# The last 64 rows of the first MLP matrix: one transfer of 128 partitions, or one of 96 and four of 8

## The chip, the cores and the metric

The kernel runs on one core of one Trainium2 chip. The metric is the device time of one execution in microseconds (us), the median of several runs. The profile is one further execution, recorded by the hardware profiler.

## What is computed

The reference mixes two blocks for a batch of 8 tokens with 576 features, all in bf16. A is attention for one decode step: 32 query heads on 16 key and value heads of 128, over the last 2048 of 8192 cached positions. B is an MLP with a hidden width of 4608. A gate per token weighs the two.

```
q = (x @ wq)                            # wq 576 x 4096
p = softmax(q . k / sqrt(128))          # k: last 2048 positions of the cache
a = (p . v) @ wo                        # wo 4096 x 576
h = gelu(layernorm(x) @ w1 + b1)        # w1 576 x 4608
b = h @ w2 + b2                         # w2 4608 x 576
g = sigmoid((x * gate_w).sum(-1))
out = g * a + (1 - g) * b
```

The two caches' windows are 134 MB of the 154 MB that the kernel reads; the weights are the rest.

## The kernel before

**Loads.** Every load is issued by SP (SyncE), on one DMA queue, in an order written out in the code by `after=` links. First come the last 64 rows of wq, its first 512 rows, x, gate_w, b1 and b2 (lines 407 to 413). Then comes w1: the 512 first rows as `d_w1m` (line 416; 128 partitions of 36,864 bytes), and the 64 last rows as `d_w1r` (line 417). For the latter each row is cut into two halves, which makes 128 pieces of 2304 elements, 4608 bytes, one per partition of the tile `w1_r`. Behind these stand the loads of the attention: 16 units, each with a K load and a V load of 4 MB (line 618), into four buffer slots used in turn. Slots 1 and 2 are free from the start, so K0 and K1 are issued right behind w1; V0 goes to slot 0, which holds wq until `q_pe` has read it, and K2 to slot 3, which holds w1 until `h_pe` has read it. At the end come w2 in four pieces (line 865) and wo in two (line 836).

**Semaphores.** A load adds 16 to its semaphore when it has landed in full. Both w1 loads use the semaphore "w1"; `h_pe`, the matmuls of the hidden layer (line 551, with its own lines 543 and 501), waits for both.

**Compute.** `q_pe` multiplies x by wq, and VectorE and ScalarE turn q into a block form. `mask0` (line 687, emitted at lines 685 and 175) writes the first unit's mask to PSUM, and `h_pe` makes the hidden layer. For each unit, VectorE transposes K (line 718), TensorE makes scores (lines 732 and 175), VectorE takes the maximum (line 645), ScalarE the exponential (line 649), and TensorE multiplies by V (lines 755 and 188). After all units the group of matmuls at line 579 adds the products with w2 and wo into one bank; line 900 copies it out and line 903 stores it.

**The order on each engine** is set by a planner (`schedule`, line 62). It holds a cost for each operation and a model of the loads, and always takes the operation that could start first. In the model, loads of at least 65,536 bytes follow each other at 428e3 bytes per us and land 1.8 us after their last byte. A smaller one on SP lands 1.8 us after what was booked so far, and books nothing itself:

```
                if op.nbytes < 65536:
                    op.t1 = (max(est + 0.4, dma_free) if op.eng == "sp" else est + 0.4) + self.DMA_LAT
                else:
                    start = max(est + 0.4, dma_free)
                    dma_free = start + op.nbytes / self.DMA_BW
                    op.t1 = dma_free + self.DMA_LAT
```

In that model h_pe can start at 25.71, and mask0, which needs the last of the q copies (line 537), at 25.44. These are the planner's own figures, which order the instructions and measure nothing.

Of the kernel before, what the change touches and what calls it, by code (L numbers as in the profile page):

```python
# [38 lines left out]
class _Plan:  # L39
# [16 lines left out]
    def dma(self, eng, fn, semkey, nbytes, deps=(), name=None, after=(), prio=0):  # L56
        op = _Op(eng, fn, deps, name, self.DMA_ISSUE, after=after, is_dma=True, dma_sem=semkey, nbytes=nbytes, prio=prio)
        op.idx = len(self.all)
        self.all.append(op)
        return op  # L60
# [134 lines left out]
def build_kernel(nc, A_x, A_k_cache, A_v_cache, A_wq, A_wo, B_x, B_w1, B_b1, B_w2, B_b2, gate_w, out):  # L195
# [3 lines left out]
    F = B_w1.shape[1]  # L199
# [25 lines left out]
    with ExitStack() as es:  # L225
# [134 lines left out]
        w1_r = RAW[:, W1O + 4 * F:W1O + 4 * F + F // 2]  # L360
# [19 lines left out]
        add, dma = P.add, P.dma  # L380
# [33 lines left out]
        dx = [d_x]  # L414
        db = [d_b1]
        d_w1m = dma("sp", lambda e: e.dma_start(w1_m.rearrange("p t c -> p (t c)"), B_w1[0:512, :].rearrange("(p t) c -> p (t c)", t=4)), "w1", 512 * F * 2, name="d_w1m", after=[d_b2])
        d_w1r = dma("sp", lambda e: e.dma_start(w1_r, B_w1[512:576, :].rearrange("k (s c) -> (k s) c", s=2)), "w1", 64 * F * 2, name="d_w1r", after=[d_w1m])  # L417
        dw1 = [d_w1m, d_w1r]


        def spread(name, src):
# [171 lines left out]
        M_CUTS = [[24], [8, 3, 1]]  # L593
        stream += [("M", 0), ("W", 0), ("W", 1), ("M", 1)]

        last_dma = [d_w1r]
        slot_free = [[o_qp], [], [], [o_hp], [o_qp, o_hp]]
        n_slot = [0]
        qk_hist, pe_hist, dve_ops = [], [], {}
# [313 lines left out]
def bass_gated_mix__sliding_block_cached__mixer_channel_mlp__decode_kernel(  # L913
    nc: bass.Bass,
    A_x: bass.AP,
    A_k_cache: bass.AP,
    A_v_cache: bass.AP,
    A_wq: bass.AP,
    A_wo: bass.AP,
    B_x: bass.AP,  # L920
    B_w1: bass.AP,
    B_b1: bass.AP,
    B_w2: bass.AP,
    B_b2: bass.AP,
    gate_w: bass.AP,
    out: bass.AP,
):
    build_kernel(nc, A_x, A_k_cache, A_v_cache, A_wq, A_wo, B_x, B_w1, B_b1, B_w2, B_b2, gate_w, out)
# [28 lines left out]
```

## Time and profile before

| what | before |
|---|---|
| median of three runs | 364.71 us (364.57 to 365.15) |
| the profiled execution, its time and its span | 364.42 us, 363.0 us |
| TensorE, VectorE, ScalarE, GpSimd busy | 81%, 64%, 46%, 6% of the span |
| bytes moved, mean rate | 154.45 MB, 425 GB/s |
| K loads: count, KB each, median from issue to landing | 16, 4096 KB, 28.7 us |
| V loads: the same | 16, 4096 KB, 25.5 us |
| d_w1m: issue, KB | 3.00 us, 4608 KB |
| d_w1r: issue, KB, issue to landing | 3.40 us, 576 KB, 23.0 us |

The page of the profile gives times in us from the start of the span. Its second part cuts the span into 40 slices and gives for each the busy tenths of an engine; the DMA line is the mean of the core's sixteen DMA engines. Its third part lists the DMA queues. The other views used below are the chain of work that ended last, in order of time; the instructions in order of time (start, duration, engine, line, operation, and in brackets how long the engine stood idle before it and what released it); and the view of one line of the code. The trace also holds two lists below these views: each DMA packet with its start, duration and size, and each step that a DMA made on a semaphore.

### The profile page before, as it was taken

Reading aid. Unit: us, or ns where it says so; the run is one execution under the profiler, and the core shown is the slowest. Engines: PE = TensorE matmul, PEld = TensorE weight load, DVE = VectorE, ACT = ScalarE, POOL = GpSimd, SP = SyncE. Lnnn points to the kernel's source line nnn. Section 1 sums busy time; section 2 is a strip of 40 time slices with the busy share of each in tenths; the row PEclk is TensorE's granted clock in tenths of the full one; section 3 lists DMA queues with packets and bytes.
Section 4 is the critical chain, followed back from the end, with each engine's and each line's share of the span. In section 5 each row is a group of like instructions: output and inputs, shape, how many; then the busy total and the mean of one; then the engine's idle time right before and its main releaser. Section 6 shows DMA issues by size and latency. Waiting matters only on the chain.

```text
span 363.0 us, 4802 instructions
## 1 busy us (share of the span) xinstructions
PE 295.1 (81%) x1935; PEld 125.4 (35%) x1423; DVE 231.6 (64%) x166; ACT 168.6 (46%) x130; POOL 22.9 (6%) x52
## 2 busy tenths in 40 slices
PE   0455357999999969898897979897979699999875
PEld 0121000435252615242433416150615143436742
DVE  0453989576666694929385768566675949295720
ACT  1022106655647464564637373838374636655000
POOL 9032030000010000000100000000000000003000
PEclk9999596999999999999999999999999989999999
DMA  8999999999999999999999999999999999999996
GB/s 347 436 437 406 459 408 459 408 459 408 454 412 455 412 455 410 452 415 451 415 451 415 446 419 448 419 448 417 448 419 448 419 446 419 448 419 444 409 434 249
DMA packets 6118, 154.45 MB, mean 425 GB/s; under 512 B 702, under 2 KB 856, under 8 KB 1244
## 3 DMA queue, kind: packets, MB, share of 16 engines
q1 hardware_dynamic: 6092, 154.30, 98.8%
q8 instruction: 8, 0.13, 0.1%
q14 instruction: 2, 0.02, 0.0%
q10 hardware_dynamic: 16, 0.00, 0.0%
HBM read 154.29 MB, written 0.01 MB: 425 GB/s over the span
## 4 chain that ended last, share of the span: by engine, by line
DMA 54%; PE 21%; DVE 21%; issue 2%; SPq 1%; ACT 0%
DMA arena<-in_A_k_cache_dram 48%; DVE arena L718 17%; PE ps L175 9%; PE ps L188 6%; DMA arena<-in_B_w_dram 6%; PE ps L732 3%; PE ps L755 2%; DVE arena L668 2%; DVE arena L645 1%; DVE arena L794 1%; PE ps L579 0%; PE ps L685 0%; DVE arena L561 0%; DVE arena L900 0%; SPq L417 0%
## 5 line engine op out<-in xcount | busy, mean ns | idle before, releaser
L718 DVE STREAM_TRANSPOSE arena<-arena 128x4096 f32<-128x4096 f32 (+1 forms) x34 | 141.7, 4175 | 24.3 <-DMA arena<-in_A_k_cache_dram 24.3
L674 ACT ACTIVATE arena<-arena 32x2048 bf16<-32x2048 bf16 x60 | 114.5, 1908 | 72.8 <-DVE arena L668 44.7
L175 PE MATMUL ps<-arena 128*128 128x512 bf16 (+3 forms) x524 | 134.7, 397 | 12.6 <-DVE arena L718 9.6
L188 PE MATMUL ps<-arena 128*128 x840 | 109.8, 277 | 6.9 <-issue 0.7
L188 PEld LDWEIGHTS ps<-arena 128*128 x840 | 81.3, 97 | 34.4 <-issue 19.1
L645 DVE TENSOR_REDUCE arena<-ps 128x1 f32<-128x2048 f32 x16 | 36.7, 2292 | 53.3 <-PE ps L175 53.3
L732 PE MATMUL ps<-arena 128*128 128x512 bf16 x122 | 48.2, 395 | 20.0 <-DVE arena L718 18.3
L732 PEld LDWEIGHTS ps<-arena 128*128 128x128 bf16 x128 | 12.5, 98 | 133.0 <-issue 75.2
L649 ACT ACTIVATE arena<-ps,arena 128x2048 bf16<-128x2048 f32 x16 | 40.6, 2538 | 0.5
L646 ACT ACTIVATE arena<-arena 128x1 f32<-128x1 f32 x16 | 3.2, 203 | 62.8 <-DVE arena L645 62.8
L755 PE MATMUL ps<-arena 128*128 128x256 bf16 x184 | 25.3, 273 | 1.2 <-DVE arena L663 1.1
L755 PEld LDWEIGHTS ps<-arena 128*128 128x128 bf16 x184 | 16.8, 98 | 19.1 <-issue 14.7
L668 DVE STREAM_TRANSPOSE arena<-arena 128x1024 f32<-128x1024 f32 x15 | 18.1, 1205 | 2.9 <-ACT arena L649 2.9
L579 PE MATMUL ps<-arena 128*8 128x288 bf16 (+1 forms) x140 | 9.6, 286 | 4.0 <-DMA arena<-in_A_wo_dram 3.3
L739 POOL MEMSET arena<- 128x4096 f32 x1 | 3.5, 3512 | 148.2 <-PE ps L175 148.2
L629 POOL COPY arena<-arena 32x64 bf16<-32x64 bf16 x16 | 3.7, 230 | 123.6 <-PE ps L175 122.7
L901 ACT ACTIVATE arena<-ps 8x288 bf16<-8x288 f32 x1 | 0.4, 401 | 19.5 <-PE ps L579 19.5
L422 DVE COPY arena<-arena 8x128 bf16<-8x128 bf16 x2 | 0.5, 229 | 13.9 <-DMA arena<-in_A_x_dram 13.9
L579 PEld LDWEIGHTS ps<-arena 128*8 128x8 bf16 (+1 forms) x140 | 5.8, 86 | 9.5 <-DMA arena<-in_A_wo_dram 3.3
L685 PE MATMUL ps<-arena 128*128 128x512 bf16 x11 | 4.4, 399 | 5.2 <-ACT arena L649 5.2
L900 DVE CAST arena<-ps 8x288 bf16<-8x288 f32 x1 | 0.4, 446 | 12.3 <-PE ps L579 12.3
L794 DVE SCALAR_TENSOR_TENSOR arena<-ps,arena 128x256 f32<-128x256 f32 x12 | 5.7, 476 | 2.8 <-PE ps L755 2.7
(105 smaller groups left out, 89.7 us busy)
## 6 DMA issues: line engine op xcount, KB each, us to landing
arena<-in_A_k_cache_dram SPq DMA_DIRECT2D x16, 4096.0 KB, 28.7
arena<-in_A_v_cache_dram SPq DMA_DIRECT2D x16, 4096.0 KB, 25.5
arena<-in_B_w_dram SPq DMA_DIRECT2D x1, 4608.0 KB, 22.0
arena<-in_A_wo_dram SPq DMA_DIRECT2D x2, 2304.0 KB, 23.8
arena<-in_A_wq_dram SPq DMA_DIRECT2D x1, 4096.0 KB, 12.6
arena<-in_B_w_dram SPq DMA_DIRECT2D x1, 3456.0 KB, 24.1
arena<-in_B_w_dram SPq DMA_DIRECT2D x1, 1152.0 KB, 22.3
arena<-in_B_w_dram SPq DMA_DIRECT2D x1, 576.0 KB, 23.0
```

What stands on the lines that cost most here:

```text
L175: return e.add_instruction(mybir.InstMatmult(name=nc.get_next_instruction_name(), engine=mybir.EngineType.PE, ins=[e.lower_ap(rhs), e.lowe ...
L188: return e.add_instruction(mybir.InstMatmult(name=nc.get_next_instruction_name(), engine=mybir.EngineType.PE, ins=[rhs, lhsT], outs=[e.low ...
L579: ins = e.matmul(ps[32 * j:32 * j + 8, BK_ACC, 0:JN], lhsT, rhs[:, JN * j:JN * j + JN], start=False, stop=True, skip_group_check=True, til ...
L645: mx = add("dve", lambda e: e.tensor_reduce(out=k(g, MX + x), in_=scores, axis=AXL.X, op=ALU.max), deps=[qk_unit[t]], name="mx%d" % t, cos ...
L649: ex = add("act", lambda e: e.activation(out=bass.AP(arena, offset=aoffs("P"), ap=[[AST, 128], [64, 32], [1, 2], [2, 32]]), in_=ps[:, 0:4, ...
L668: pc = add("dve", lambda e: e.transpose(view("PC").bitcast(F32), view("P").bitcast(F32)), deps=[ex] + (sp_done[t - 1][0] if t else [o_acc0 ...
L674: return e.activation(out=bass.AP(arena, offset=32 * a * AST + aoffs(home) + 64 * a, ap=[[AST, 32], [256, 32], [1, 64]]), in_=bass.AP(aren ...
L685: mm = e.matmul(*args, start=True, stop=False, skip_group_check=True) if n == 0 else held_matmul(nc, e, *args, start=True, stop=False, ski ...
L718: return e.transpose(bass.AP(arena_f, offset=foffs(base) + 2048 * h0, ap=[[AST // 2, 128], [1, 2048 * nh]]), bass.AP(arena_f, offset=foffs ...
L732: mm = e.matmul(*args, start=False, stop=True, skip_group_check=True) if rc == 0 else held_matmul(nc, e, *args, stop=True, skip=True)
L755: return e.matmul(dst, bass.AP(arena, offset=aoffs(home) + 256 * q + ee, ap=[[AST, 128], [2, 128]]), slot(s).rearrange("p (r k d) -> p r k ...
L794: fn = lambda e, src=src, w=w: e.scalar_tensor_tensor(out=X2, in0=src, scalar=w, in1=X2, op0=ALU.mult, op1=ALU.add)
```

## The change

The second w1 load becomes five loads on the same queue and the same semaphore, one behind the other: partitions 0 to 95, and then 96 to 103, 104 to 111, 112 to 119 and 120 to 127. The same bytes go to the same places. `h_pe` depends on all of them and on `d_w1m`, and the first K load is ordered behind the last of them.

```diff
-        d_w1r = dma("sp", lambda e: e.dma_start(w1_r, B_w1[512:576, :].rearrange("k (s c) -> (k s) c", s=2)), "w1", 64 * F * 2, name="d_w1r", after=[d_w1m])
-        dw1 = [d_w1m, d_w1r]
+        d_w1r = [d_w1m]
+        for p0, p1 in ((0, 96), (96, 104), (104, 112), (112, 120), (120, 128)):
+            d_w1r.append(dma("sp", (lambda p0=p0, p1=p1: lambda e: e.dma_start(w1_r[p0:p1, :], B_w1[512:576, :].rearrange("k (s c) -> (k s) c", s=2)[p0:p1, :]))(),
+                             "w1", (p1 - p0) * F, name="d_w1r%d" % p0, after=d_w1r[-1:]))
+        dw1 = d_w1r
...
-        last_dma = [d_w1r]
+        last_dma = d_w1r[-1:]
```

The sizes that the planner is given are 442,368 bytes for the first of the five and 36,864 for each of the other four.

## The prediction

> **What bounds the kernel now.** I read the page first, for the share of each engine.
>
> ```profile
> PE 295.1 (81%) x1935; PEld 125.4 (35%) x1423; DVE 231.6 (64%) x166; ACT 168.6 (46%) x130; POOL 22.9 (6%) x52
> ...
> DMA  8999999999999999999999999999999999999996
> ...
> q1 hardware_dynamic: 6092, 154.30, 98.8%
> q8 instruction: 8, 0.13, 0.1%
> ```
>
> The sixteen DMA engines are busy from the first slice to the last (98.8% of 16 engines' span), and no compute engine is. Then the view of line 618, which issues the K and V loads, and the end of the chain in order of time:
>
> ```profile
> DMA to landing us min/median/max: 19.1/27.6/42.4
> ```
>
> ```profile
> 333.37 3.53 PE ps L755 x32
> 336.90 0.02 issue
> 336.92 22.33 DMA arena<-in_B_w_dram
> 359.25 0.04 issue
> 359.30 1.71 PE ps L579 x24
> 361.03 0.45 DVE arena L900
> ```
>
> Each buffer slot is loaded every fourth time, and the landings on one slot's semaphore are 38.7 us apart (35.3, 74.1, 112.8 for slot 1), so a load of 4 MB takes 9.7 us; from issue to landing it needs 19.1 us at least. So at least 9.4 us of other loads always stand ahead of it. The chain ends with a wait for the last pieces of the second MLP matrix. What counts is when the **slowest DMA engine** has moved its own bytes: TensorE's last matmuls wait for the last engine's landing.
>
> So I went to the trace's packet records (start, duration, bytes, but no engine's name). A packet of one engine starts 4 ns before the recorded end of the one before it, so the packets link into sixteen chains from 13 us to the end. The row packet of 4608 bytes takes 178 ns and starts 174 ns after the last; the closing 4-byte semaphore packet adds 6 ns. A chain has 8 rows of w1_r. The engines of the transfer of x (8 partitions) are known by its 1152-byte packets at 12.94 to 13.08 us: eight chains have one. Call these the **low eight**, the rest the **high eight**. The four chains with b1's 2304-byte packets (4 partitions) are all among the low eight, and the chain with the one-partition loads is among those four: few partitions always mean the same first engines.
>
> Each of the 8 packets of queue q8 (16 KB of instructions, 0.88 to 0.96 us each) holds up one chain, by 0.91 us and 0.5 us more on its next packet: some 1.42 us. They fell on eight different chains, and those are the late ones at the end:
>
> ```
> end of the last data packet, us (start of the fetch that hit the chain)
> low eight   358.46 358.53 358.55 358.93 359.04 359.38   359.85 (297.6) 359.87 (249.2)
> high eight  358.72 (one more not followed past 209)     359.91 (336.2) 359.94 (349.5) 360.00 (31.5)
>                                                         360.02 (144.1) 360.03 (98.1) 360.11 (199.8)
> ```
>
> The sixteen landings of the last load show the same two groups: eight from 358.73 to 359.69, eight from 360.20 to 360.40.
>
> **The change part by part.**
>
> *Bytes per engine.* I take it that 96 partitions go six to an engine and each transfer of 8 goes one to each of the low eight. Low: 6 + 4 = 10 rows for 8, which is 2 x 174 ns, and four closing packets of 6 ns more: +0.37 us. High: 6 rows for 8, -0.35 us. All chains run without gaps, so this shift is carried to the end. The latest low chain goes from 359.87 to 360.24, the latest high one from 360.11 to 359.76. The slowest engine thus changes sides, and the end moves by 360.24 - 360.11 = **+0.13 us**; the landing follows its data by 0.29 to 0.35 us, which lets me take +0.15. No row shows a load of 96 partitions. Bounds: on sixteen engines as above; if on eight only, +1.2 us (below); if all late chains were high ones, -0.35 us.
>
> [...]
>
> *Issue on SP.* The row of the present load and the K loads behind it:
>
> ```profile
> 3.00 0.36 SPq L416 DMA_DIRECT2D arena<-in_B_w_dram  x1
> 3.40 0.43 SPq L417 DMA_DIRECT2D arena<-in_B_w_dram  x1
> 3.87 1.25 SPq L618 DMA_DIRECT2D arena<-in_A_k_cache_dram  x2
> 19.57 0.54 SPq L618 DMA_DIRECT2D arena<-in_A_v_cache_dram  x1
> ```
>
> Four more issues at 0.37 us (x's row) and 0.04 us between: K0 and K1 are issued 1.6 us later, at 5.5 us. The first chain needs K0 at 25.3 us and V0's issue waits for TensorE until 19.57, so 19.8 and 12.4 us cover it: cost nothing. Without that cover it would be 1.6 us.
>
> *The fixed toll of a transfer.* On seven of the low chains small transfers follow one another with those 6 ns and no gap. On the first engine it is more: its one-partition bias load took 152 ns for 51, and the next packet 1546 for 1364, so 0.28 us at worst. Bounds 6 ns and 0.28 us each; I take 6 ns, since three of four small packets even on that engine show it, and keep the other end as a rival.
>
> *h_pe's wait and the planner.* h_pe waits for all six loads on one semaphore instead of two. Now:
>
> ```profile
> 25.70 1.49 PE L175 MATMUL ps<-arena 128*128 128x512 bf16 x3 [1.71 <-ACT arena L536]
> 27.12 1.14 PE L543 MATMUL ps<-arena 4*128 4x384 bf16 x3
> ```
>
> The last w1_r landing is at 26.13, and mask0 holds TensorE until 27.12. With +0.37 the landing is at 26.50: still under mask0. But the planner (line 98) books no bandwidth for loads under 64 KB: 4 x 36,864 bytes at 428e3 per us leave its sum, 0.34 us, so for it h_pe is ready at 25.36, not 25.71, ahead of mask0 at 25.44. I expect the two to swap: h_pe would start some 0.27 us after the landing (the delay of the first VectorE work on x, 13.62 to 13.89), at 26.8, and end 0.3 us earlier. Queued behind it are the bias matmuls and mask0, which would end near 34 us; mask0's user, the first scores, starts at 41.8 us, after K0's landing (37.02) and a transpose of 4.45 us. K2's issue (now 32.29, after h_pe) also comes 0.3 us earlier. All of it is hidden by the loads; uncovered, a late h_pe would cost 0.4 us. A small swap of the same kind may follow in the first softmax group; under 9.4 us of queue it costs nothing.
>
> **Sum.** The profiled execution took 364.42 us, its span 363.0; +0.15 gives 364.57. The median of the three runs is 364.71 (364.57 to 365.15), which the predicted time refers to: 364.71 + 0.15 = **364.86 us**.
>
> **Rivals.**
> 1. *The late engines are all high ones in most runs.* The instruction fetches could fall on other chains than in this profile, or I linked two chains wrongly. Then the end follows the high eight: -0.35 us, 364.36. For it: six of eight fetches did hit high chains. Against: from K0's first row until their fetch the two late low chains never came within 2 ns of another, so the linking holds for them, and the fetches come from a program that hardly changes. Chance 0.2.
> 2. *A toll per small transfer, the other side.* If each 8-partition load cost its engines the first engine's 0.28 us, the low eight would lose 4 x 0.28 = 1.1 us beside 0.37: 359.87 + 1.49 = 361.36, against 360.11 +1.25, so 366.0. It decides from a toll of 0.15 us on. For it, that one chain; against, the seven others. [...] Chance 0.06.
> 3. *The 96 partitions use only eight engines,* so the change doesn't do what it says: the low eight get 12 + 4 = 16 rows, 8 x 174 ns + 24 ns = +1.42 us, an end of 361.29, +1.2 us, 365.9. For it: no such load is in the trace. Against: every load here splits as its count divides. Chance 0.02.
> 4. *An instruction fetch moves onto a chain that has had one.* The longer SP program or the swapped order could do it: +1.42 us, 366.1. Against: eight fetches, eight chains. Chance 0.03.
> 5. *Something faster that no row shows,* over 0.7 us. Chance 0.04.
>
> My forecast keeps 0.65. A measurement of this kernel can tell some 0.2% (0.73 us) from no change. The forecast and rival 1 lie within it; 2, 3 and 4 make 0.11 of slower, rival 5 is faster. The range: the forecast with the spread of the runs before reaches 365.2, and rival 1 with the same spread 364.2.
>
> **What would show it.** Right: the sixteen landings of w1's rest in two groups some 0.7 us apart, eight early and eight late; at the end the late fetched low chains last, and the last landing 0.1 to 0.2 us later against the fetches. A last landing 0.35 us earlier means rival 1; gaps behind the 4-byte packets of the low chains mean rival 2; rows of 96 on eight chains mean rival 3; a chain with two 16 KB packets rival 4. TensorE's order around 26 us shows whether the planner swapped. The forecast is wrong if a load's landing falls under 10 us from issue, since then the engines run dry.

## The result, and the profile after

The changed kernel takes 366.66 us (median of six runs, 366.50 to 367.06), the kernel before 364.74 us (six runs beside them, 364.57 to 365.15). The ratio is 1.0053, with a 95% interval of 1.0040 to 1.0066: 1.92 us slower, half a percent. The forecast was 364.86 us in a range of 364.2 to 365.2. The profiled execution took 366.67 us, its span 365.1 us.

The page of the changed kernel: the busy shares, the DMA engines by slice, the GB/s by slice and the queue.

```profile
PE 295.5 (81%) x1954; PEld 124.7 (34%) x1423; DVE 231.4 (63%) x166; ACT 168.6 (46%) x130; POOL 22.9 (6%) x52
...
DMA  8999999999999999999999999999999999999995
GB/s 345 433 373 404 431 434 431 434 434 431 435 425 445 424 438 429 432 434 427 438 427 445 425 438 424 442 427 429 434 434 434 431 440 424 438 431 431 422 427 240
...
q1 hardware_dynamic: 6124, 154.30, 98.7%
```

The GB/s line of the kernel before:

```profile
GB/s 347 436 437 406 459 408 459 408 459 408 454 412 455 412 455 410 452 415 451 415 451 415 446 419 448 419 448 417 448 419 448 419 446 419 448 419 444 409 434 249
```

The engines work as long as before and the DMA engines are as busy as before. What moved is the third slice, 18.3 to 27.4 us: 373 GB/s, where it was 437. So the DMA engines are busy but move less there; that is when w1's last rows are loaded. The same stretch of 8 us as a row of its own (busy time by engine, granted clock, DMA share, GB/s), first of the kernel before, then of the changed one:

```profile
22.00:30.00 8.00, 5.34 (x34) 1.24 (x20) 1.93 (x8) 1.59 (x6) 4.20 (x19) 1.00 0.96 410
```

```profile
22.00:30.00 8.00, 2.17 (x11) 0.78 (x11) 2.12 (x8) 1.59 (x6) 4.20 (x19) 0.50 0.96 311
```

The DMA share is 0.96 in both. The missing 99 GB/s over 8 us are 0.79 MB, which at the mean 425 GB/s take 1.9 us: the whole loss sits in this stretch. The end of the chain is the same work in nearly the same lengths, all of it 2.0 to 2.2 us later:

```profile
339.07 0.02 issue
339.09 22.19 DMA arena<-in_B_w_dram
361.27 0.04 issue
361.32 1.75 PE ps L582 x24
363.07 0.02 issue
363.09 0.45 DVE arena L903
```

SP's issues in order of time, and the hidden layer:

```profile
3.21 0.36 SPq L416 DMA_DIRECT2D arena<-in_B_w_dram  x1
3.61 1.83 SPq L419 DMA_DIRECT2D arena<-in_B_w_dram  x5
```

```profile
28.86 1.13 PE L546 MATMUL ps<-arena 4*128 4x384 bf16 x3 [4.68 <-DMA arena<-in_B_w_dram]
...
34.84 0.64 PE L582 MATMUL ps<-arena 1*8 1x288 bf16 x4
35.41 0.39 PE L688 MATMUL ps<-arena 128*128 128x512 bf16 x1
```

The five issues take 1.83 us, and K0 is issued at 5.47 us. The hidden layer now stands ahead of mask0 (line 688 here) and waits 4.7 us for w1, until 28.86 us: the last of w1's landings is at 28.81, where it was at 26.37 (both counted from the start of the span, as on the page).

The packet records say how. Linked into chains as for the prediction, the durations (ns) of the 4608-byte rows and of the first K0 packets are as follows. (In the jam several packets start within a few ns of each other, so the last four rows of the low chain could belong to another of the low eight; rows and K0 packets of that kind look alike in all of them. Of the 128 rows before, two took 202 and 216 ns.)

```
before, every chain     178 178 178 178 178 178 178 178                   K0 1213 1213 1213
after, one of the high  178 178 178 293 301 302                           K0 2626 1227 1216
after, one of the low   178 178 178 288 306 299 307 321 459 425           K0 1821 1213 1213
```

Around 24.8 us (24.6 to 25.0) all sixteen chains slow down together, while all of them are still in the transfer of 96. The rows take up to 474 ns, and the first K0 packet of the high eight, which have no 8-partition transfer at all, takes 2.5 to 2.7 us instead of 1.2. The extra time of the rows is 12.0 us over sixteen chains, that of the first K0 packets 16.8 us: (12.0 + 16.8) / 16 = **1.81 us for each engine**. After the first two K0 packets of each chain they take 1213 to 1219 ns again, but for the one behind an instruction fetch. The landings lag as well: the last of w1's comes 1.10 us after the end of its last data packet, where it came 0.35 us after it before.

The K0 landings, counted from the mean landing of the first 512 rows of wq, show the shift of bytes on top of it:

```
before  21.93 to 22.42 (fifteen)                                23.62 (the one with a fetch)
after   23.45 to 23.92 (seven)    24.14 to 24.52 (eight)        25.20 (the one with a fetch)
```

### The profile page after: what moved, and what is told of

Read it like the earlier page. It is cut to its first block, busy times and chain, and to the rows that moved or that the text cites. A ratio compares the mean times of both kernels' runs of the same rounds, so it can differ in the third digit from the quotient of the medians.

```text
span 365.1 us, 4826 instructions
## 1 busy us (share of the span) xinstructions
PE 295.5 (81%) x1954; PEld 124.7 (34%) x1423; DVE 231.4 (63%) x166; ACT 168.6 (46%) x130; POOL 22.9 (6%) x52
## 4 chain that ended last, share of the span: by engine, by line
DMA 52%; PE 23%; DVE 22%; issue 1%; SPq 1%; ACT 0%
DMA arena<-in_A_k_cache_dram 39%; DVE arena L721 18%; DMA arena<-in_B_w_dram 13%; PE ps L175 9%; PE ps L188 6%; PE ps L735 3%; PE ps L758 2%; DVE arena L671 2%; DVE arena L648 1%; PE ps L582 0%; PE ps L504 0%; DVE arena L560 0%; SPq L419 0%; ACT arena L558 0%; PE ps L546 0%
## 5 line engine op out<-in xcount | busy, mean ns | idle before, releaser
L735 PE MATMUL ps<-arena 128*128 128x512 bf16 x128 | 50.5, 395 | 28.6 <-DVE arena L721 26.9
L758 PEld LDWEIGHTS ps<-arena 128*128 128x128 bf16 x184 | 16.8, 99 | 19.0 <-issue 14.8
L688 PE MATMUL ps<-arena 128*128 128x512 bf16 x16 | 6.3, 393 | 5.2 <-ACT arena L652 5.2
L560 DVE TENSOR_TENSOR arena<-arena 128x1152 f32<-128x1152 f32 x1 | 1.4, 1359 | 11.4 <-ACT arena L558 11.4
L903 DVE CAST arena<-ps 8x288 bf16<-8x288 f32 x1 | 0.4, 447 | 12.4 <-PE ps L582 12.4
```

Source lines behind the costliest of these rows:

```text
L688: mm = e.matmul(*args, start=True, stop=False, skip_group_check=True) if n == 0 else held_matmul(nc, e, *args, start=True, stop=False, ski ...
L735: mm = e.matmul(*args, start=False, stop=True, skip_group_check=True) if rc == 0 else held_matmul(nc, e, *args, stop=True, skip=True)
L758: return e.matmul(dst, bass.AP(arena, offset=aoffs(home) + 256 * q + ee, ap=[[AST, 128], [2, 128]]), slot(s).rearrange("p (r k d) -> p r k ...
```

## The experiments

Theories, guesses of mine for the runs to choose between. *Destination*: neighbouring partitions share a way into the on-chip memory, and a transfer that puts several engines on one way at a time jams them and whoever comes behind. *Toll*: each small transfer costs its engines a fixed time. *Source*: engines that read neighbouring rows collide. *Order*: the planner's new order costs the time. A "way", here and in the expectations, is a word of the first theory alone: no trace shows one, nor how many there would be, nor which partitions would share one; and none shows which engine writes which partition. All times are medians beside runs of the kernel before on the same chip. In e2, e3 and e9 the hidden layer gets its rows in another order than the weights have, so these three compute something else; only their time is compared. The extra packet time is that of the rows and the first two K0 packets of each engine, over sixteen.

| kernel | against before, us | ratio, 95% interval | extra packet time, us an engine |
|---|---|---|---|
| changed kernel | +1.92 | 1.0053 (1.0040 to 1.0066) | 1.81 |
| e1_96_32 | +0.80 | 1.0023 (1.0014 to 1.0033) | 0.83 |
| e2_dst_step | +1.43 | 1.0039 (1.0025 to 1.0053) | 1.26 |
| e3_src_step | +2.08 | 1.0052 (1.0035 to 1.0068) | 1.96 |
| e4_tiny | +0.46 | 1.0011 (1.0000 to 1.0021) | 0.01 |
| e5_order | -0.02 | 0.9998 (0.9988 to 1.0007) | 0.00 |
| e6_own | +0.61 | 1.0015 (1.0005 to 1.0024) | 0.51 |
| e8_halves | +1.14 | 1.0029 (1.0018 to 1.0040) | 1.32 |
| e9_inter | -0.05 | 0.9999 (0.9990 to 1.0009) | 0.06 |
| e10_shift | +0.56 | 1.0012 (1.0003 to 1.0022) | 0.33 |
| e11_tiny16 | +2.26 | 1.0061 (1.0047 to 1.0074) | 0.72 (1.71 over all of K0) |
| e12_more_near | +1.80 | 1.0053 (1.0040 to 1.0067) | 1.07 |
| e13_more_own | +0.43 | 1.0012 (1.0003 to 1.0021) | 0.04 |

### Order alone

```diff
-..., "w1", 64 * F * 2, name="d_w1r", after=[d_w1m])
+..., "w1", 96 * F, name="d_w1r", after=[d_w1m])
```

> The kernel before, with the loads as they were, but the planner is told 442,368 bytes for the last rows. It then orders the engines as in the changed kernel: h_pe ahead of mask0, and two small operations of the first softmax group moved. If the new order costs the time: 1 us slower or more. If the loads bound the time, as both the prediction and the destination theory hold: within 0.3 us of before.

No difference (within 0.4 us by the interval). The order theory falls, and the order that the prediction put at nothing costs nothing that can be measured.

### Source against destination

In both kernels the transfers of the changed kernel keep their number and size; one side of the 8-partition transfers is spread.

```diff
# e2: write every fourth partition, read neighbours
+w1_r[96 + j:128:4, :]          <- rows 96 + 8 * j to 103 + 8 * j
# e3: read every fourth half row, write neighbours
+w1_r[96 + 8 * j:104 + 8 * j]   <- rows 96 + j, 100 + j, ... 124 + j
```

> As the changed kernel, but each 8-partition transfer writes every fourth partition (96+j, 100+j, ... 124+j) in place of 8 neighbours; it still reads 8 neighbouring rows. The hidden layer thus gets the last 32 half rows in another order. Destination theory: the 8 engines no longer share two ways, so about half of the loss goes: 0.5 to 1.3 us slower than before instead of 1.9. Toll theory: the same number of transfers, so 1.9 us slower as the changed kernel. Source theory: the same rows are read together, 1.9 us slower.

> As the changed kernel, but each 8-partition transfer reads every fourth half row; it still writes 8 neighbouring partitions. The hidden layer thus gets the last 32 half rows in another order. Destination theory: 1.9 us slower than before, as the changed kernel. Source theory: most of the loss goes, under 0.8 us slower. Toll theory: 1.9 us slower.

Spreading the reads changes nothing (+2.08): the source theory falls. Spreading the writes helps, by 0.5 us, less than I expected (+1.43 against 0.5 to 1.3); the intervals of the two times overlap, but the packet time falls as well, from 1.81 to 1.26 us. The first K0 packets of the high eight still take 2.1 us. Why is not shown; with the small rows on 0 to 31 in place of 96 to 127 (e13 below) these packets stay at 1213 ns.

### Two transfers, no small ones

```diff
# e1                       # e8                        # e9
+w1_r[0:96]                +w1_r[0:64]                 +w1_r[0:128:2]
+w1_r[96:128]              +w1_r[64:128]               +w1_r[1:128:2]
```

> The 128 rows as a transfer of 96 partitions and one of 32, two transfers in place of five; the order on the engines is that of before. In the changed kernel the packets of 4608 bytes take 300 to 460 ns instead of 178 from 24.6 us on, while the 96 is still being moved, and the first K0 packets up to 2.6 us instead of 1.2; together 28.8 us over sixteen engines, 1.8 us each. Destination theory: partitions that lie close together share one way into the memory, and both transfers put several engines on one way; the 96 already jams, so slow packets from 24.6 us again, and 0.5 to 1.2 us slower than before. Toll theory (each small transfer costs its engines about 0.4 us): one extra transfer only, at most 0.4 us slower, and rows of the 96 at 178 ns. Source theory (engines reading neighbouring rows of the matrix collide): little left without the 8s, within 0.3 us of before.

> The 128 rows as two transfers of 64 neighbouring partitions, 0 to 63 and 64 to 127; the order on the engines is that of before, no small transfer and no shift of bytes between engines. Destination theory: each half reaches only half of the ways into the memory with all sixteen engines, so its packets take twice the time: packets of 4608 bytes near 350 ns, 1.39 us more for 8 rows an engine, 1.0 to 1.6 us slower than before. Toll theory: one transfer more, at most 0.4 us slower.

> The same two transfers of 64 partitions with the same reads, but the first writes the even partitions and the second the odd ones. The hidden layer thus gets its last rows in another order. Destination theory: both now reach all ways, so less than half of the loss of the contiguous halves: 0 to 0.7 us slower than before. If it is the number of partitions or of transfers that costs: as slow as the contiguous halves.

The pair of e8 and e9 is the cleanest: the same two reads of 64 half rows, the same issues, the same share for each engine, the same order. With neighbours it costs 1.14 us, with every second partition nothing. The row of 22 to 30 us, of e8 and then of e9:

```profile
22.00:30.00 8.00, 4.16 (x15) 0.93 (x12) 2.02 (x8) 1.59 (x6) 4.19 (x19) 1.00 0.98 345
```

```profile
22.00:30.00 8.00, 5.61 (x35) 1.19 (x20) 2.06 (x8) 1.59 (x6) 4.20 (x19) 0.50 0.97 410
```

410 GB/s is what the kernel before moves there. TensorE's granted clock in these rows, 1.00 and 0.50, is not the cause: the kernel with 0.50 is the one that loses nothing. In e8 the rows take 340 to 360 ns at the worst, twice the 178. Sixteen engines with 4608 bytes in 345 ns move 214 GB/s, half of the 424 that they move with a row every 174 ns. That is the rate that the destination theory expected of a contiguous half; its reason, half of the ways, was a guess, while that the place of the writes decides is shown. e1 says that 96 neighbours and then 32 jam as well, with no small transfer in it: +0.80 us.

### The small transfers

e6 keeps the 96 and the four 8s and only changes where they write. e12 and e13 leave the transfer of 128 whole and add four more, of the same size as those of the change.

```diff
# e6: 96 to 32:128, the 8s to every fourth of 0:32
+w1_r[32:128]; w1_r[j:32:4], j = 0..3
# e12: whole transfer, and four copies to neighbours
+free[96 + 8 * j:104 + 8 * j], j = 0..3
# e13: whole transfer, and four copies to every fourth
+free[j:32:4], j = 0..3
```

> As the changed kernel in number and size of transfers, planner and order, but the 96 goes to partitions 32 to 127, and each of the four 8-partition transfers writes every fourth partition of 0 to 31, so that the eight engines each write to a group of four partitions of their own. Destination theory: the 8s cost nothing beyond their bytes and the high engines' K0 is free of them, so only the jam of the 96 is left: 0.4 to 1.0 us slower than before, first K0 packets below 1.8 us. Toll theory: 1.9 us slower as the changed kernel.

> The kernel before with its one transfer of 128 partitions, and four more transfers of 8 neighbouring partitions of 4608 bytes (a second copy of the last 32 half rows, partitions 96 to 127, to a free place), which the hidden layer waits for; the order on the engines is that of before. The first eight engines move 4 rows more, 0.72 us. Destination theory: the neighbours jam as in the changed kernel, without the 96: slow first K0 packets above 2 us on the other eight engines, all K0 landings 0.9 to 1.5 us later and those of the first eight 0.7 us later still; 1.5 to 2.3 us slower than before. Toll theory at four transfers (some 0.1 us each, by the tiny ones): K0 packets near 1.2 us on the other eight, 0.5 to 1.1 us slower.

> The same four more transfers, of the same size, but to every fourth partition of 0 to 31 (a second copy of these half rows), so that each of the eight engines writes to a group of four partitions of its own. Destination theory: no jam; rows near 178 ns, the other eight engines' K0 untouched, the first eight 0.72 us later, of which some 0.5 us shows at the end with up to 0.4 us of toll: 0.4 to 1.0 us slower than before. If only the number and size of the transfers count: the same as with the neighbours.

e12 and e13 have the same number, size and engines. (e13 also reads every fourth half row, which by e3 changes nothing.) With neighbours: +1.80 us; with every fourth partition of 0 to 31: +0.43 us. The row of 22 to 30 us, of e12 and then of e13:

```profile
22.00:30.00 8.00, 4.48 (x19) 0.92 (x12) 2.02 (x8) 1.59 (x6) 4.22 (x19) 0.55 0.97 354
```

```profile
22.00:30.00 8.00, 5.59 (x35) 1.17 (x20) 2.08 (x8) 1.59 (x6) 4.20 (x19) 0.50 0.95 403
```

In e12 the added rows take up to 478 ns and the first K0 packets of the high eight 2.2 to 2.4 us; in e13 nearly all rows take 178 ns and the high eight's K0 packets 1213. In e13 the low eight's K0 lands 22.61 to 23.05 us after wq, seven of the others at 21.94 to 22.26: 0.7 us apart, the 4 rows at 174 ns that were added, and no toll. At the end of the run that makes 359.87 + 0.72 - 360.11 = 0.48 us, and 0.43 was measured. e6 agrees: with the 8s on every fourth partition of 0 to 31, +1.92 us becomes +0.61.

Two things differ between e12 and e13, the spread of the writes and their place, 96 to 127 against 0 to 31. No run sends small transfers of full-size rows to neighbours on 0 to 31, and e2 shows that the spread alone is not enough on 96 to 127. So it is shown that the partitions written decide, and not which of the two matters how much.

### Tiny transfers

```diff
+for j in range(4):     # e11: range(16), over all partitions
+    dma("sp", free[96 + 8 * j:104 + 8 * j, 256 elements] <- B_w1[...], "w1", 8 * 512, ...)
```

> The kernel before, with its one transfer of 128 partitions, and four more transfers of 8 partitions of 512 bytes to a free place behind it, which the hidden layer waits for; the order on the engines is that of before. Toll theory: most of the 1.9 us comes back, 1.2 us slower or more. Destination and source theories: the bytes are few, so within 0.3 us of before.

> As the kernel with four small transfers of 8 partitions of 512 bytes, but with sixteen of them, over all partitions. There the four gave 0.5 us with an interval from 0 to 0.8. Toll theory, if that was real: four times as much, about 1.8 us slower. Destination theory: only the bytes and the closing packets count, 16 x some 34 ns on the first eight engines, of which 0.3 us shows at the end: 0 to 0.5 us slower.

Four tiny transfers leave the packets alone, and their 0.46 us is above the 0.3 that I expected, but at the edge of what can be told from nothing; the execution that was profiled is the fastest of them (364.31 us), so its trace can't show where the 0.46 would lie. Sixteen cost 2.26 us, as the toll theory had it and against mine. The packets pass in some 30 ns each, and the last of them ends at 26.57 us. But the closing semaphore steps of the eight engines come some 0.2 us apart on each, until 29.60 us, 3.0 us behind the data, and the first K0 packets of eight chains take 2.3 to 2.8 us.

That looks like a toll of about 0.2 us behind the packets. But e11's transfers also write neighbours, and the lag of the last landing behind its data goes with neighbours elsewhere too: 0.95 us in e4, 1.03 in e12, 1.07 in e8, and only 0.42 in e13 and 0.34 in e9 (e10, with spread writes and 0.80 us, does not fit as well). No run has tiny transfers on spread partitions, so it stays open how much of e11's loss is a toll and how much the destination.

### The shift alone

e10 cuts the 128 rows into a transfer of the 64 even partitions, one of 32 and four of 8. By the split that the changed kernel shows, eight engines move 10 of these rows and the others 6, as there, and every transfer writes spread partitions.

```diff
+w1_r[0:128:2]; w1_r[1:128:4]; then w1_r[3 + 32 * j:32 + 32 * j:4], j = 0..3
```

> [...] Prediction's step alone: packets stay near 178 ns, and the time is 0.1 to 0.2 us above before, which can't be told from no change. If six transfers, or the uneven share, cost the time: 1.9 us slower, as the changed kernel.

+0.56 us: far from the 1.9, and above the 0.1 to 0.2 of the shift, which the interval (0.1 to 0.8 us) just reaches. The rows are near 178 ns (0.9 us extra over all), but first K0 packets take up to 1.5 us, 4.4 us extra over all: 0.33 us an engine. With the shift of 0.13 that makes 0.46. Why the spread writes still disturb K0 a little is open; e10's small transfers go to 3 to 127, where those of e13, which leave K0 alone, stay within 0 to 31. No version tried beats the kernel before.

## Why the prediction was wrong

**What bounds the kernel: right.** The engines that compute are as busy as before, and the time follows the DMA engines: the extra packet time, with 0.13 us for the shift where there is one, gives 1.94 us for the changed kernel's 1.92, 1.39 for e2's 1.43, 2.09 for e3's 2.08, 0.64 for e6's 0.61 and 0.46 for e10's 0.56; without a shift 0.83 for e1's 0.80, 1.32 for e8's 1.14 and 0.06 for e9's -0.05. For e12 and e13, whose shift is 0.48 us, it gives 1.55 for 1.80 and 0.52 for 0.43. These are means over the engines, and good to the width of the intervals, some 0.4 us either way. The tiny transfers lie above it: 0.01 for e4's 0.46, and 0.72 for e11's 2.26, or 1.71 with all of K0.

**The split over engines: right.** That 96 partitions go six to an engine was taken without a run that showed it. In the changed kernel the w1 semaphore shows 68 steps: sixteen each for the 512 rows and for the 96, and one early and eight later for each small transfer. (In the kernel before, x's 8 partitions show one early step and eight later ones, b1's 4 partitions one and four, and w1's two loads of 128 sixteen each.) Rival 3 is out. The chains have 6 and 10 rows, and the two groups of K0 landings are some 0.6 us apart, where 0.72 was forecast. A shift of this size was there; the 0.13 us at the end can't be told from noise by itself. Of the last load's landings two come last and alone, at 362.54 and 362.72 us behind seven from 362.00 to 362.25, as the forecast had it for two late low chains; which engines they belong to was not followed to the end.

**The price of a row, in "Low: 6 + 4 = 10 rows for 8, which is 2 x 174 ns": this step failed.** "All chains run without gaps, so this shift is carried to the end" holds as far as it goes: there are no gaps, and the shift is there. But I gave every row of the new transfers 174 ns, the distance in a transfer over all 128 partitions, left K0's packets at their old length, and bounded the 96 only by the number of engines, never by the place that they write to. From about the fourth row on the rows take 250 to 470 ns, and the following load's first packets up to 2.7 us, also on engines that the change took bytes away from. The term measured 1.81 us an engine where I had none; it is nearly all of the 1.92 us.

**A price of cutting the load: given too little weight.** Beside the bytes and the four closing packets the sum has no term for it. That the parts share engines is not what costs: in e8 and e9 the parts share the same sixteen engines, and only e8 loses (+1.14 us against -0.05). What e8 against e9 and e12 against e13 (+1.80 us against +0.43) show is that the partitions written at a time decide.

**Rival 2, a toll per small transfer, had the right sign, and its 366.0 us is 0.7 short, for another reason.** (Rivals 3 and 4, at 365.9 and 366.1, came as near, and neither is what happened.) It put the loss on the low eight. The high eight lost as much: their K0 landings are 1.6 us later although they have 0.35 us less to move. Four transfers of the same size cost nothing beyond their bytes in e13, so their number is not what costs; whether a toll is part of e11's loss is open.

**SP's issues: right** (K0 at 5.47 us for 5.5; the cover before V0's issue is 12.8 us by the rows shown, 19.57 less 5.12 and 1.6, and not 12.4). **The planner's swap: right** in the order, also in the first softmax group; wrong in its times, since h_pe started 2.1 us later than forecast (28.86 for 26.8). The prediction also set two scales side by side there: its packet and landing times lie 0.24 us too early against the page. On the page's scale x's last landing is at 13.87 us, so VectorE's work at 13.89 follows it by 0.02 us and not by 0.27. The two slips cancel (26.37 + 0.37 + 0.02 = 26.76), and nothing in the sum hung on them. e5 shows that the order costs nothing. **Rivals 1 and 4** are not the cause: the loss is there in full when K0 lands, and up to then one fetch has hit one chain in both kernels (at 31.8 us before, at 34.4 us after).

## What to carry to other kernels

When a transfer is cut by partitions, ask of each part not only how many engines move it but which partitions they write to at a time. Eight neighbours in each small transfer (e12, +1.80 us), or a contiguous half of the partitions in a big one (e8, +1.14 us), slowed the stretch of 22 to 30 us here to 354 and 345 GB/s, where the kernel before moves 410. The same half spread over every second partition was free (e9, -0.05 us); small parts spread over every fourth cost no more than their bytes on 0 to 31 (e13, +0.43 us where the bytes make 0.48), but helped little on 96 to 127 (e2, +1.43 us against 1.92 with neighbours), so the spread has to be measured with the load behind it. A DMA share that stays the same (0.96) while the GB/s fall in one stretch (410 to 311) was the sign here, and the packet durations there say the rest (rows of 178 ns before, up to 474 ns after).

## What the runs showed of the hardware that I had not expected

- A 4608-byte packet takes 178 ns in the transfer over all 128 partitions (126 of the 128 rows before) and in e9's over every second one, 340 to 360 ns at the worst when sixteen engines write 64 neighbouring partitions (e8), and up to 478 ns with eight engines on 8 neighbours (e12).
- The jam reaches engines that have no part in the small transfers: their next 32 KB packet takes 2.5 to 2.7 us for 1.2 in the changed kernel, and 2.2 to 2.4 us in e12.
- It builds up: in the changed kernel the first two to four rows of nearly every chain still take 178 ns, and then all sixteen slow down around 24.8 us.
- It shows in the landings too: the last of w1's comes 0.34 to 0.42 us after its data in the kernel before, e5, e9 and e13, and 0.7 to 1.1 us after it in the changed kernel and the other kernels with full-size rows.
- After sixteen tiny transfers in a row, whose packets take 27 ns, the closing steps come some 0.2 us apart on each engine, and the last is 3.0 us behind the data.
